# A windowed-attention and SwiGLU kernel on one core: loads reordered, later values cast by their DMA, attention steps on a fixed grid

## The chip, the cores and the metric

The kernel runs on one core of one Trainium2 chip. The metric is the device time of one execution in microseconds (us). Before the change three runs gave 435.56, 435.69 and 436.59 us; the median is 435.69 us.

## The reference

Eight batches of eight heads, 576 positions of 64 elements. Each query sees the keys within 32 positions, the eight positions in `global_idx` see all keys and are seen by all queries. The output rows of the attention go through a gated feed-forward block (FFN).

```python
scores = scale * np.matmul(q, k.transpose(0, 1, 3, 2))
mask = np.abs(pos[:, None] - pos[None, :]) <= 32
mask = mask | is_global[:, None] | is_global[None, :]
attn = softmax(np.where(mask, scores, -1e9))
x = np.matmul(attn, v).transpose(0, 2, 1, 3).reshape(4608, 512)
g = x @ w_gate
out = ((g / (1 + np.exp(-g))) * (x @ w_val)) @ w_out
```

## The kernel before

All matmuls are in bf16. The program writes its instructions in the order in which each engine executes them; each engine takes its own in that order, and a semaphore wait holds everything behind it on that engine.

**FFN.** The 4608 tokens are taken in nine chunks of 512. A chunk is 16 units: twelve `gate` units (four matmuls of 128x512 with `wg_sb` into `pg`, four with `wv_sb` into `pv`, a tanh on ScalarE, two products on VectorE) and four `outp` units (twelve matmuls with `wo_sb` into `po`, a scaling on ScalarE, a store). The operand is `xT`, which the attention fills.

**Attention.** A batch is a list of steps. `step_T` (batches 0 and 1 alone) transposes a pair of heads of the loaded `k_bf`, `q_bf` on TensorE into `kT`, `qT`. `step_GT`, `step_S2`, `step_SG`, `step_P2T`, `step_AV2` treat the global rows and columns: they need `kqm`, the gathered rows of the eight global positions. `step_S(u)` computes a band of scores, its exponential (ScalarE) and its product with the band mask (VectorE, `pt`). `step_AV(tp)` multiplies 128 rows of probabilities with the values (`va`, and `vb`, the values shifted by 64 rows, and `gvt` from `step_AV2`) and normalises on VectorE; `step_X(tp)` transposes the result into `xT`. `step_AV8` and `step_X8` do the last 64 rows.

**PSUM.** `psc` (tag "sc") and `pm` (tag "m") hold one pair of banks each, `pf` (tag "f") four single banks. `step_S`, `step_S2`, `step_SG` use `psc`; `step_AV` uses `pm`.

**Loads.** GpSimd issues the DMAs that cast from fp32 to bf16: `k_bf`, `q_bf`, the weights, and from batch 2 on `cast_qk`, which writes `kf`, `qf` to DRAM. It also issues the indirect gathers `kg`, `qg`, and `gather_mask` multiplies these into `kqm`. Each DMA of GpSimd waits for its eighth predecessor to land. The values come through SyncE as fp32 (`load_v` into `vst`) and GpSimd casts them (`cast_v`, line 108) into `va_bufs[b % 2]`. SyncE also issues `transpose_qk` (DMA transposes of `kf`, `qf` into `kT`, `qT`, lines 122 and 126), `load_vb` (lines 133, 134, a copy of `va` to `vb`) and the output stores (line 630).

**Order around the change.** The opening (lines 652 to 657) is batch 0 but for its last three steps. Then each chunk c takes the steps of batch c + 1, and `interleave` spreads them over the chunk by the units' estimated durations; `cast_qk`, `transpose_qk`, `load_v`, the gather and `cast_v` of later batches hang on units 1, 3, 5, 6 and 9 of each chunk.

Of the kernel before, what the change touches and what calls it, by code (L numbers as in the profile page):

```python
# [17 lines left out]
P = 128  # L18
# [8 lines left out]
def kernel(  # L27
# [63 lines left out]
    def v_block(u):  # L91
        return (WIN if u == 0 else 0), (P - WIN if u == 4 else P), P * u - WIN

    def load_v(b):
        vst = ldp.tile([P, 5, H, D], FP32, tag="vst", name="vst")
        vs = v[b].rearrange("h s d -> s h d")
        r = []
        for u in range(5):
            lo, hi, t0 = v_block(u)
            r.append(nc.sync.dma_start(out=vst[lo:hi, u], in_=vs[t0 + lo : t0 + hi]))  # L100
        return vst, r

    def cast_v(b, vst):
        va = va_bufs[b % 2]
        for u in range(5):
            lo, hi, _ = v_block(u)
            for a, z in ((lo, 64), (64, hi)) if u == 0 else ((lo, hi),):
                nc.gpsimd.tensor_copy(out=va[a:z, u, :, 0:D], in_=vst[a:z, u])  # L108

    flat = {}  # L110

    def cast_qk(b):
        for name, src in (("k", k), ("q", q)):
            t = dram.tile([S, H, D], BF16, name=f"{name}f{b}")
            nc.gpsimd.dma_start(out=t, in_=src[b].rearrange("h s d -> s h d"))
            flat[name, b] = t
# [116 lines left out]
    def gather_mask(kg, qg):  # L233
        kqm = gw.tile([P, 2, 2, D], BF16, tag="kqm", name="kqm")
        for a, src in ((0, kg), (1, qg)):
            nc.gpsimd.tensor_tensor(
                out=kqm[:, a], in0=bc(src, [[0, 2], [1, D]]),
                in1=bc(mka[:, a, :], [[1, 2], [0, D]]), op=ALU.mult,
            )
        return kqm  # L240

    vsts = [None] * B
    vsts[0], ins = load_v(0)
    for f in first:
        tc.add_manual_dep(
            ins[0].ins, f.ins.name,
# [10 lines left out]
    def load_wgv(i):  # L257
# [15 lines left out]
        out=band, in_=band, compare_op=ALU.is_ge, fill=0.0,  # L273
        base=2 * WIN, pattern=[[1, 64]], channel_multiplier=-1,
    )
    kqms[0] = gather_mask(*g0)
    cast_v(0, vsts[0])
    load_wgv(0)
    load_wgv(1)
    loaded[1] = new_qk()  # L280
    load_qk_part(1, loaded[1], 0)
    load_qk_part(1, loaded[1], 1)
    load_wgv(2)
    for i in range(4):
        nc.gpsimd.dma_start(
            out=wo_sb[:, 3 * i : 3 * i + 3, :],
            in_=moe_w_out[3 * P * i : 3 * P * (i + 1), :].rearrange("(fc p) m -> p fc m", p=P),
        )
    kqms[1] = gather_mask(*gather(1))


    mg = const.tile([P, S], BF16)
# [28 lines left out]
    def attention(b):  # L321
# [11 lines left out]
        def step_T(hp):  # L333
            if hp == 0:
                qTs[b] = bp.tile([P, HP, S], BF16, tag="qT", name="qT")
            if b > 0:
                pair = pm.tile([P, 2, 1024], BF16, tag="m", name="ps_t")
            for n, name in enumerate(("k", "q")):
                if b == 0:
                    ps = pf.tile([P, LJ, LP], BF16, tag="f", name="ps_t")  # L340
                else:
                    ps = pair[:, n, 0:S].rearrange("p (j i) -> p j i", j=LJ)
                src = ld[name]
                for j in range(LJ):
# [212 lines left out]
        def vb():  # L557
            st["vb"] = load_vb(b)

        L = lambda f, *a: (lambda: f(*a))  # L560
        if b == 0:
            return [
                L(step_T, 0), L(step_T, 1), tables, L(step_S, 0), L(step_T, 2), L(step_T, 3),
                L(step_GT), L(step_S2), L(step_SG), vb, L(step_P2T), L(step_S, 1),
                L(step_AV2), L(step_S, 2), L(step_AV, 0), L(step_S, 3), L(step_X, 0),
                L(step_AV, 1), L(step_X, 1), L(step_AV, 2), L(step_X, 2), L(step_AV, 3),
                L(step_X, 3),
            ], [[L(step_S, 4)], [L(step_AV8)], [L(step_X8)]]
        if b == 1:
            head = [  # L570
                [L(step_T, 0)], [L(step_T, 1)], [L(step_T, 2), vb], [L(step_T, 3)],
                [L(step_GT)],
            ]
        else:
            head = [[L(step_GT), vb]]
        return [], head + [
            [L(step_S2)],
            [L(step_SG)],
            [L(step_P2T), L(step_S, 0)],
# [58 lines left out]
    def interleave(units, steps):

        total = sum(d for d, _ in units)  # L640
        t = 0.0
        i = 0
        for d, f in units:
            f()
            t += d
            while i < len(steps) and (i + 0.5) * total <= t * len(steps):
                for g in steps[i]:
                    g()
                i += 1
        assert i == len(steps)  # L650

    head, rest = attention(0)
    for f in head:
        f()
    vsts[1], _ = load_v(1)
    cast_v(1, vsts[1])
    cast_qk(2)
    for c in range(NT // CH):
        steps = rest
        rest = []  # L660
        if c + 1 < B:
            steps += attention(c + 1)[1]
        units = ffn(CH * c, CH)

        def at(i, f, *a):
            d, g = units[i]
            units[i] = (d, lambda: (g(), f(*a)))

        if c + 2 < B:
            def raw(b):  # L670
                vsts[b], _ = load_v(b)

            def rows(b):
                kqms[b] = gather_mask(*gather(b))

            if c + 3 < B:
                at(1, cast_qk, c + 3)
            at(3, transpose_qk, c + 2)
            at(5, raw, c + 2)
            at(6, rows, c + 2)  # L680
            at(9, lambda b: cast_v(b, vsts[b]), c + 2)
        interleave(units, steps)


# [28 lines left out]
```

## Time and profile before

| | us |
|---|---|
| median of three runs | 435.69 |
| the profiled execution's own time | 433.27 |
| its span, first to last instruction | 431.6 |
| busy: TensorE, VectorE, ScalarE, GpSimd | 361.5, 238.9, 161.8, 96.3 |

A row of the profile names the source line, the engine (PE is TensorE, PEld its weight loads, DVE VectorE, ACT ScalarE, POOL GpSimd, SPq the queue of SyncE), the operation and the tiles as out<-in. The 40 digits of a slice line cover the span in equal parts of 10.8 us. PEclk is the granted TensorE clock: 1.00 is 2.4 GHz and 0.50 is 1.2 GHz. The difference between the own time and the span, 1.7 us, lies outside of the instructions.

### The profile page before, as it was taken

The page shows a single profiled execution, that of the slowest core. Times are in us where ns is not written, and L with a number is a line of the kernel's source. Part 1 is how long each engine was busy: PE and PEld are TensorE (multiplying, and loading weights), DVE is VectorE, ACT ScalarE, POOL GpSimd, SP SyncE. Part 2 cuts the span into 40 slices and gives each one's busy share as a digit, 9 for nine tenths or more (in the row PEclk, how much of TensorE's full clock was granted, in tenths as well). Part 3 has the DMA queues.
Part 4 walks back from the last instruction along what each step waited for, and adds up shares of the span by engine and source line. Part 5 has one row for each costly group of instructions (what it writes and reads, how often), then busy time and mean ns, then how long its engine had stood idle before and what let it go on. Part 6 is the DMA issues. An engine that isn't in the chain of part 4 may idle for free. (4 is left out here: it accounts for less than half of the span.)

```text
span 431.6 us, 7877 instructions
## 1 busy us (share of the span) xinstructions
PE 361.5 (84%) x3221; PEld 180.3 (42%) x3274; DVE 238.9 (55%) x467; ACT 161.8 (37%) x258; POOL 96.3 (22%) x122
## 2 busy tenths in 40 slices
PE   2668758028799989899899899898989998999996
PEld 2443323014344444454455444444444454444442
DVE  6554637004278538853884488358826862871760
ACT  3432424004354436333542355345435542322321
POOL 6642148127108200710270033003000000000000
PEclk9999979559999999999999999999999999999999
DMA  8999949998995939794989590168012001002002
GB/s 128 149 191 192 199 86 110 158 200 88 177 200 71 120 99 199 75 123 116 211 58 116 130 190 8 71 146 152 2 73 76 2 3 73 24 0 97 2 1 97
DMA packets 136147, 45.47 MB, mean 105 GB/s; under 512 B 122544, under 2 KB 130224, under 8 KB 136112
## 3 DMA queue, kind: packets, MB, share of 16 engines
q0 software_dynamic: 63968, 14.68, 36.3%
q1 hardware_dynamic: 72144, 30.29, 33.2%
q8 instruction: 25, 0.41, 0.4%
q14 instruction: 10, 0.08, 0.1%
HBM read 38.28 MB, written 16.52 MB: 127 GB/s over the span
## 5 line engine op out<-in xcount | busy, mean ns | idle before, releaser
L604 PE MATMUL pg<-xT,wg_sb 128*128 128x512 bf16 x402 | 109.9, 387 | 3.8 <-issue 2.2
L604 PE MATMUL pv<-xT,wv_sb 128*128 128x512 bf16 x425 | 111.8, 385 | 0.2
L610 ACT ACTIVATE th<-pg 128x512 bf16<-128x512 f32 x108 | 64.6, 598 | 115.2 <-PE pg L604 102.7
L612 DVE SCALAR_TENSOR_TENSOR gv<-th,pg 128x512 bf16<-128x512 bf16 x108 | 74.0, 685 | 56.0 <-ACT th L610 55.8
L623 PE MATMUL po<-wo_sb,h 128*128 128x512 bf16 x416 | 95.3, 379 | 2.2 <-issue 2.1
L616 DVE TENSOR_TENSOR h<-gv,pv 128x512 bf16<-128x512 bf16 x108 | 74.3, 688 | 11.8 <-PE pv L604 0.8
L604 PEld LDWEIGHTS <-wv_sb 128*128 128x128 bf16 x432 | 42.9, 99 | 52.8 <-issue 3.2
L623 PEld LDWEIGHTS <-h 128*128 128x128 bf16 x432 | 40.0, 98 | 45.6
L108 POOL CAST va<-vst 128x512 bf16<-128x512 f32 (+3 forms) x48 | 31.2, 659 | 122.2 <-DMA vst<-in_v_dram 88.9
L628 ACT ACTIVATE osb<-po 128x512 f32<-128x512 f32 x36 | 21.5, 597 | 91.4 <-PE po L623 71.9
L604 PEld LDWEIGHTS <-wg_sb 128*128 128x128 bf16 x432 | 37.3, 99 | 42.5 <-issue 7.0
L465 DVE TENSOR_TENSOR pt<-pe,band 128x1024 bf16<-128x1024 bf16 (+1 forms) x40 | 26.0, 651 | 35.3 <-ACT pe L460 35.2
L460 ACT ACTIVATE pe<-ps_s 128x1024 bf16<-128x1024 f32 (+1 forms) x40 | 37.8, 944 | 9.6 <-PE ps_s L452 9.6
L477 DVE TENSOR_REDUCE den<-ps_av 128x8 f32<-128x16 f32 (+1 forms) x40 | 6.8, 170 | 60.0 <-PE ps_av L504 37.8
L504 PE MATMUL ps_av<-vb,pt 128*64 128x66 bf16 x256 | 18.6, 202 | 19.9 <-DMA vb<-va 19.9
L504 PEld LDWEIGHTS <-pt 128*64 128x64 bf16 x512 | 18.6, 118 | 20.4 <-DMA vb<-va 18.9
L483 DVE TENSOR_TENSOR xa<-ps_av,den 128x512 bf16<-128x512 f32 (+1 forms) x40 | 25.5, 638 | 1.4
L541 ACT COPY xT<-ps_x 128x512 bf16<-128x512 bf16 x32 | 18.7, 583 | 18.5 <-PE ps_x L535 18.5
L495 PE MATMUL ps_av<-gvt,pg 128*64 128x264 bf16 x128 | 18.8, 305 | 7.6 <-DVE gvt L437 7.3
L535 PE MATMUL ps_x<-ident,xa 128*128 128x128 bf16 x128 | 13.4, 231 | 7.0 <-DVE xa L483 7.0
L504 PE MATMUL ps_av<-va,pt 128*64 128x66 bf16 x256 | 18.8, 202 | 0.0
L452 PE MATMUL ps_s<-qT,kT 64*128 64x64 bf16 x576 | 16.3, 197 | 1.8 <-DVE mg L311 1.0
(92 smaller groups left out, 224.0 us busy)
## 6 DMA issues: line engine op xcount, KB each, us to landing
out_dram<-osb SPq DMA_DIRECT2D x36, 256.0 KB, 2.0
vst<-in_v_dram SPq DMA_DIRECT2D x24, 256.0 KB, 6.3
vb<-va SPq DMA_DIRECT2D x16, 264.0 KB, 4.0
kf<-in_k_dram POOLq DMA_DIRECT2D x6, 576.0 KB, 8.3
qf<-in_q_dram POOLq DMA_DIRECT2D x6, 576.0 KB, 10.9
vst<-in_v_dram SPq DMA_DIRECT2D x16, 192.0 KB, 5.5
wg_sb<-in_moe_w_gate_dram POOLq DMA_DIRECT2D x3, 512.0 KB, 12.8
wv_sb<-in_moe_w_val_dram POOLq DMA_DIRECT2D x3, 512.0 KB, 15.4
```

The lines of the kernel that those rows point to most:

```text
L108: nc.gpsimd.tensor_copy(out=va[a:z, u, :, 0:D], in_=vst[a:z, u])
L460: nc.scalar.activation(out=pe, in_=ps[:, :, 0 : 64 * ns].rearrange("p r (s c) -> p r s c", c=64), func=AF.Exp, scale=SCALE,)
L465: nc.vector.tensor_tensor(out=pt.rearrange("p r s c -> p (r s) c"), in0=pe.rearrange("p r s c -> p (r s) c"), in1=bc(band, [[0, 2 * ns], [ ...
L483: nc.vector.tensor_tensor(out=xa.rearrange("p (g h) d -> p g h d", g=g), in0=bc(ps, pst + [[1, D]]), in1=bc(den, [[4, g], [1, 4], [0, D]]) ...
L495: nc.tensor.matmul(out=ps[64 * e : 64 * e + 64, hg], lhsT=st["pg"][:, P * tp + 64 * e : P * tp + 64 * e + 64], rhs=st["gv"].rearrange("p h ...
L504: nc.tensor.matmul(out=ps[64 * e : 64 * e + 64, hg, hl, :], lhsT=pt[:, hl % 2, 4 * (hl // 2) + 2 * (tp % 2) + e, :], rhs=(va if e == 0 els ...
L604: nc.tensor.matmul(out=ps[:, 0:n], lhsT=w[:, cc, P * fc : P * (fc + 1)], rhs=xT[:, cc, t0 : t0 + n], start=(cc == 0), stop=(cc == NCC - 1),)
L610: nc.scalar.activation(out=th[:, 0:n], in_=pg[:, 0:n], func=AF.Tanh, scale=0.5)
L612: nc.vector.scalar_tensor_tensor(out=gv[:, 0:n], in0=th[:, 0:n], scalar=1.0, in1=pg[:, 0:n], op0=ALU.add, op1=ALU.mult,)
L616: nc.vector.tensor_tensor(out=st["h"][:, fc, 0:n], in0=gv[:, 0:n], in1=pv[:, 0:n], op=ALU.mult)
L623: nc.tensor.matmul(out=po, lhsT=st["h"][:, fc, P * ts : P * (ts + 1)], rhs=wo_sb[:, fc, :], start=(fc == 0), stop=(fc == NFC - 1),)
L628: nc.scalar.mul(out=osb, in_=po, mul=0.5)
```

## The change

The values of batch 0 keep their way (`load_v0`, `cast_v0`), but the first gather mask and two weight loads stand between the casts. From batch 1 on `load_v` is five DMAs on GpSimd's queue that cast on the way into `va_bufs`; `vst` and the GpSimd casts are gone there. The gather of batch 1 is issued ahead of the second weight pair, `load_v(1)` behind the third, `cast_qk(2)` behind the output weights. `step_T` of batch 1 takes its PSUM pair from `psc` for three of four head pairs, and odd `step_AV` of batch 0 take theirs from `psc`. The opening runs all four `step_S` of batch 0 ahead of `step_GT`. `interleave` is replaced by a table `gaps`: gap n stands behind unit n of the whole program, and one step (a few pairs) goes into each; batch 1 fills gaps 0 to 15, batches 2 to 7 follow from gap 16 on at a pitch of 1.14 units.

```diff
+    def cast_v0(vst, us):
+        for u in us:
...
+    def load_v(b):
+        va = va_bufs[b % 2]
+        vs = v[b].rearrange("h s d -> s h d")
+        for u in range(5):
+            lo, hi, t0 = v_block(u)
+            nc.gpsimd.dma_start(out=va[lo:hi, u, :, 0:D], in_=vs[t0 + lo : t0 + hi])
...
+    cast_v0(vst0, range(0, 3))
     kqms[0] = gather_mask(*g0)
-    cast_v(0, vsts[0])
+    cast_v0(vst0, range(3, 4))
     load_wgv(0)
+    cast_v0(vst0, range(4, 5))
+    g1 = gather(1)
     load_wgv(1)
     loaded[1] = new_qk()
     load_qk_part(1, loaded[1], 0)
     load_qk_part(1, loaded[1], 1)
+    kqms[1] = gather_mask(*g1)
     load_wgv(2)
+    load_v(1)
...
-    kqms[1] = gather_mask(*gather(1))
+    cast_qk(2)
...
-                pair = pm.tile([P, 2, 1024], BF16, tag="m", name="ps_t")
+                pool, tag = (pm, "m") if hp == 3 else (psc, "sc")
+                pair = pool.tile([P, 2, 1024], BF16, tag=tag, name="ps_t")
...
-            full = pm.tile([P, 2, 512], FP32, tag="m", name="ps_av")
+            pool, tag = (psc, "sc") if b == 0 and tp % 2 else (pm, "m")
+            full = pool.tile([P, 2, 512], FP32, tag=tag, name="ps_av")
...
+        def later():
+
+            if b + 2 < B:
+                transpose_qk(b + 2)
+                kqms[b + 2] = gather_mask(*gather(b + 2))
+            if b + 3 < B:
+                cast_qk(b + 3)
+
+        def later_v():
+            if b + 2 < B:
+                load_v(b + 2)
...
+                L(step_T, 0), L(step_T, 1), tables, L(step_S, 0), L(step_S, 2),
+                L(step_T, 2), L(step_T, 3), L(step_S, 1), L(step_S, 3),
+                L(step_GT), L(step_S2), L(step_SG), vb, L(step_P2T), L(step_AV2),
+                L(step_AV, 0), L(step_AV, 1), L(step_X, 0), L(step_AV, 2), L(step_X, 1),
+                L(step_AV, 3), L(step_X, 2), L(step_X, 3),
+            ], [L(step_S, 4)], [L(step_AV8), later_v], [L(step_X8)]
...
-            [L(step_X, 2), L(step_S, 4)],
+            [L(step_X, 2), L(step_S, 4), later],
...
-            [L(step_AV8)],
+            [L(step_AV8), later_v],
...
+    for i, g in enumerate([s4, av8, x8, []]):
+        gaps[i] = g + tops[i]
+    for i, g in enumerate(core[:12]):
+        gaps[4 + i] = g
+    gaps[8].append(lambda: transpose_qk(2))
+    gaps[9].append(lambda: kqms.__setitem__(2, gather_mask(*gather(2))))
+    gaps[10].append(lambda: cast_qk(3))
...
+    for i, g in enumerate(order):
+        gaps[16 + int(i * 1.14)] = g
...
+        for f in ffn(c * CH, CH):
+            f[1]()
+            for g in gaps.get(n, []):
+                g()
+            n += 1
```

Three places of the order. First SyncE's queue from the values of batch 0 to the first stores, before the change (the number behind kf, qf is the batch; va0 and vb_391 belong to batch 0, va1 and vb_833 to batch 1):

```order
L133 DMA vb_391<-va0_95 64x2112
L134 DMA vb_391<-va0_95 64x2112
L100 DMA vst_619<-in_v_dram 96x8x64
L100 DMA vst_619<-in_v_dram 128x8x64 x3
L100 DMA vst_619<-in_v_dram 96x8x64
L122 DMA_TRANSPOSE kT0_97<-kf2_631 128x4x576
L126 DMA_TRANSPOSE qT_762<-qf2_633 128x4x576
L133 DMA vb_833<-va1_96 64x2112
L134 DMA vb_833<-va1_96 64x2112
```

and now, where the last va0 and vb_1417 belong to batch 2:

```order
L140 DMA vb_463<-va0_95 64x2112
L139 DMA vb_841<-va1_96 64x2112
L140 DMA vb_841<-va1_96 64x2112
L128 DMA_TRANSPOSE kT0_97<-kf2_218 128x4x576
L132 DMA_TRANSPOSE qT_1048<-qf2_220 128x4x576
L652 DMA out_0_dram<-osb_1199 128x512
L652 DMA out_0_dram<-osb_1241 128x512
L128 DMA_TRANSPOSE kT1_98<-kf3_1140 128x4x576
L132 DMA_TRANSPOSE qT_1264<-qf3_1142 128x4x576
L652 DMA out_0_dram<-osb_1290 128x512
L652 DMA out_0_dram<-osb_1332 128x512
L139 DMA vb_1417<-va0_95 64x2112
```

The shifted values of batch 1 moved ahead of the transposes of batch 2; those of batch 2 stand behind the transposes of batch 3.

Second, GpSimd from the third weight pair (`wg_sb`, `wv_sb`) to the casts for batch 2 (`kf`), before:

```order
L259 DMA wg_sb<-in_moe_w_gate_dram 128x4x512
L259 DMA wv_sb<-in_moe_w_val_dram 128x4x512
L285 DMA wo_sb<-in_moe_w_out_dram 128x3x512 x4
L226 DMA kg<-in_k_dram,gofs 128x64
L226 DMA qg<-in_q_dram,gofs 128x64
L236 TENSOR_TENSOR kqm<-kg,mka 128x128
L236 TENSOR_TENSOR kqm<-qg,mka 128x128
L108 CAST va_96<-vst 32x8x64
L108 CAST va_96<-vst 64x8x64
L108 CAST va_96<-vst 128x8x64 x3
L108 CAST va_96<-vst 96x8x64
L115 DMA kf_631<-in_k_dram 4608x1x64
```

and now (the gather of batch 1 has been issued ahead of the second weight pair):

```order
L242 TENSOR_TENSOR kqm<-kg,mka 128x128
L242 TENSOR_TENSOR kqm<-qg,mka 128x128
L264 DMA wg_sb<-in_moe_w_gate_dram 128x4x512
L264 DMA wv_sb<-in_moe_w_val_dram 128x4x512
L114 DMA va_96<-in_v_dram 96x8x64
L114 DMA va_96<-in_v_dram 128x8x64 x3
L114 DMA va_96<-in_v_dram 96x8x64
L295 DMA wo_sb<-in_moe_w_out_dram 128x3x512 x4
L121 DMA kf_218<-in_k_dram 4608x1x64
```

The mask of batch 1 moved from behind the output weights to ahead of the third weight pair, and six casts became five DMAs.

Third, ScalarE in the opening (kT copies belong to `step_T`, pe to `step_S`, p2e, pge, p2t to the global steps, xT to `step_X`), before:

```order
L296 ACTIVATE iq<-iq,ngcol 128x640
L460 ACTIVATE pe<-ps_s 128x1024
L352 COPY kT_97<-ps_t 128x576 x2
L402 ACTIVATE p2e<-ps_s_365 128x640
L384 ACTIVATE pge<-ps_sg 128x576
L416 COPY p2t<-ps_p2t 128x640
L460 ACTIVATE pe<-ps_s 128x1024 x3
L541 COPY xT<-ps_x 128x4x128 x4
```

and now:

```order
L306 ACTIVATE iq<-iq,ngcol 128x640
L471 ACTIVATE pe<-ps_s 128x1024 x2
L363 COPY kT_97<-ps_t 128x576 x2
L471 ACTIVATE pe<-ps_s 128x1024 x2
L413 ACTIVATE p2e<-ps_s_437 128x640
L395 ACTIVATE pge<-ps_sg 128x576
L427 COPY p2t<-ps_p2t 128x640
L553 COPY xT<-ps_x 128x4x128 x4
```

Three exponentials moved ahead of the global steps.

## Rows read from the trace of the kernel before

**Rows 1.** The page: its head, and the granted clock in 40 slices.

```profile
span 431.6 us, 7877 instructions
...
PEclk9999979559999999999999999999999999999999
```

**Rows 2.** Waits of TensorE, 0 to 117 us: who <- for whom: us in total, times, longest.

```profile
PE ps_av L504 <- DMA vb<-va: 19.9, 1, 19.9
PE ps_x L535 <- DVE xa L483: 7.0, 6, 1.3
...
PE ps_g L366 <- POOL kqm L236: 3.6, 1, 3.6
```

**Rows 3.** Timeline of SyncE's queue around 80 us: start, duration, instruction.

```profile
72.57 5.76 SPq L122 DMA_TRANSPOSE kT<-kf  x1
78.44 6.44 SPq L126 DMA_TRANSPOSE qT<-qf  x1
84.98 0.54 SPq L133 DMA_DIRECT2D vb<-va  x1
```

**Rows 4.** Timeline of GpSimd around 60 us; in brackets the idle time before and its end.

```profile
59.77 0.39 POOL L236 TENSOR_TENSOR kqm<-kg,mka 128x128 bf16<-128x128 f32 x1 [13.50 <-DMA kg<-in_k_dram,gofs]
...
60.59 3.85 POOL L108 CAST va<-vst 32x512 bf16<-32x512 f32 x6
64.39 2.28 POOL L115 DMA_DIRECT2D kf<-in_k_dram  x1
```

**Rows 5.** Timeline of TensorE in the opening.

```profile
14.74 0.46 PE L366 MATMUL ps_g<-ident,kqm 128*128 128x128 bf16 x2
...
22.50 0.43 PE L495 MATMUL ps_av<-gvt,pg 128*64 128x264 bf16 x2 [1.04 <-DVE gvt L437]
...
33.51 0.61 PE L535 MATMUL ps_x<-ident,xa 128*128 128x128 bf16 x4 [1.27 <-DVE xa L483]
```

**Rows 6.** Timeline of ScalarE in the opening: the first exponential.

```profile
12.78 1.02 ACT L460 ACTIVATE pe<-ps_s 128x1024 bf16<-128x1024 f32 x1 [2.92 <-PE ps_s L452]
```

**Rows 7.** Timeline of TensorE in chunks 0 and 1.

```profile
34.78 0.59 PE L604 MATMUL pg<-xT,wg_sb 128*128 128x512 bf16 x1 [0.67 <-ACT xT L541]
...
55.61 1.03 PE L604 MATMUL pv<-xT,wv_sb 128*128 128x512 bf16 x4
...
116.97 0.81 PE L604 MATMUL pg<-xT,wg_sb 128*128 128x512 bf16 x3
...
132.51 0.30 PE L495 MATMUL ps_av<-gvt,pg 128*64 128x264 bf16 x2 [0.86 <-DVE gvt L437]
```

**Rows 8.** The chain that ended last: chunk 7 begins, one pv group, chunk 8 begins.

```profile
365.34 0.86 PE pg L604 x4
366.20 0.86 PE pv L604 x4
...
396.42 0.86 PE pg L604 x4
```

**Rows 9.** Waits of TensorE, 117 to 366 us (chunks 1 to 6).

```profile
PE ps_av L495 <- DVE gvt L437: 5.6, 6, 1.2
PE ps_av L516 <- ACT xT L541: 5.6, 6, 0.9
```

**Rows 10.** One line's durations (ns min/median/max): line 437 to 30 us, then lines 437 and 465, 117 to 366 us.

```profile
L437 DVE TENSOR_TENSOR gvt<-lo,gvt x1: 195/195/195, 22.3 to 22.3; 128x8 bf16<-128x8 f32 x1
...
L437 DVE TENSOR_TENSOR gvt<-lo,gvt x6: 195/462/466, 132.0 to 339.3; 128x8 bf16<-128x8 f32 x6
...
L465 DVE TENSOR_TENSOR pt<-pe,band x30: 424/692/1062, 128.6 to 356.1; 128x1024 bf16<-128x1024 bf16 x24, 128x512 bf16<-128x512 bf16 x6
```

**Rows 11.** DMA traffic: all, 19 to 53 us; GB/s in 40 slices, 137.5 to 147.6 and 127.2 to 134.5 us.

```profile
DMA packets 10152, 6.62 MB, mean 195 GB/s; under 512 B 4894, under 2 KB 10021, under 8 KB 10149
...
GB/s 0 0 2 41 65 96 84 137 154 153 158 152 157 159 157 160 157 160 157 153 155 155 160 157 160 156 160 156 160 156 160 157 161 156 257 124 66 8 0 0
...
GB/s 209 230 220 265 271 252 324 223 223 230 222 217 218 66 15 10 15 15 36 104 180 192 252 285 251 154 97 146 180 243 237 126 84 17 15 15 10 0 0 0
```

More of the change, by code (lines that the diff above doesn't have):

```diff
@@ L92, in v_block, with load_v0 @@
         return (WIN if u == 0 else 0), (P - WIN if u == 4 else P), P * u - WIN
-    def load_v(b):
+    def load_v0():
         vst = ldp.tile([P, 5, H, D], FP32, tag="vst", name="vst")
-        vs = v[b].rearrange("h s d -> s h d")
+        vs = v[0].rearrange("h s d -> s h d")
         r = []
@@ L101, in load_v @@
         return vst, r
-    def cast_v(b, vst):
-        va = va_bufs[b % 2]
-        for u in range(5):
+    def cast_v0(vst, us):
+        for u in us:
             lo, hi, _ = v_block(u)
             for a, z in ((lo, 64), (64, hi)) if u == 0 else ((lo, hi),):
-                nc.gpsimd.tensor_copy(out=va[a:z, u, :, 0:D], in_=vst[a:z, u])
+                nc.gpsimd.tensor_copy(out=va_bufs[0][a:z, u, :, 0:D], in_=vst[a:z, u])
+    def load_v(b):
[4 more added lines that the diff above has]
+            nc.gpsimd.dma_start(out=va[lo:hi, u, :, 0:D], in_=vs[t0 + lo : t0 + hi])
     flat = {}
@@ L240, in gather_mask @@
         return kqm
-    vsts = [None] * B
-    vsts[0], ins = load_v(0)
+    vst0, ins = load_v0()
     for f in first:
@@ L562, in attention @@
             return [
[L563 to L576, printed above, removed]
+                L(step_T, 0), L(step_T, 1), tables, L(step_S, 0), L(step_S, 2),
[4 more added lines that the diff above has]
+            ], [L(step_S, 4)], [L(step_AV8), later_v], [L(step_X8)]
+        core = [
             [L(step_S2)],
@@ L585, in attention @@
             [L(step_AV, 2)],
-            [L(step_X, 2), L(step_S, 4)],
+            [L(step_X, 2), L(step_S, 4), later],
             [L(step_AV, 3)],
             [L(step_X, 3)],
-            [L(step_AV8)],
+            [L(step_AV8), later_v],
             [L(step_X8)],
         ]
+        if b == 1:
+            return [
+                [L(step_GT)], [L(step_T, 0)], [L(step_T, 1)], [L(step_T, 2), L(step_T, 3), vb],
+            ], core
+        return [[L(step_GT), vb]] + core
     def ffn(t0, n):
@@ L635, in ffn @@
         ]
[L638 to L652, printed above, removed]
+    head, s4, av8, x8 = attention(0)
     for f in head:
         f()
-    vsts[1], _ = load_v(1)
-    cast_v(1, vsts[1])
-    cast_qk(2)
-    for c in range(NT // CH):
[L659 to L682, printed above, removed]
+    tops, core = attention(1)
+    gaps = {}
+    for i, g in enumerate([s4, av8, x8, []]):
[5 more added lines that the diff above has]
+    gaps[10].append(lambda: cast_qk(3))
+    due = {1: 16}
+    order = core[12:]
+    for b in range(2, B):
+        steps = attention(b)
+        due[b] = len(order) + 2 * ((512 - 64 * b + P - 1) // P) + 4
+        order += steps
+    for i, g in enumerate(order):
+        gaps[16 + int(i * 1.14)] = g
+    for b in range(2, B):
+        assert 16 + int(due[b] * 1.14) < 16 * b, (b, due[b])
+    n = 0
+    for c in range(NT // CH):
+        for f in ffn(c * CH, CH):
[3 more added lines that the diff above has]
+            n += 1
+    assert max(gaps) < n
 _INS = ['q', 'k', 'v', 'global_idx', 'moe_w_gate', 'moe_w_val', 'moe_w_out']
```

## The prediction

> **What bounds the kernel now.** I read the head of the page and its clock line first [rows 1], then TensorE's waits in two stretches [rows 2, 9], then the timelines of the queues behind the longest wait [rows 3, 4], and last the chain that ended last [rows 8]. The chain shows that TensorE is the bound where nothing disturbs it: chunk 7, without attention, runs from 365.34 to 396.42, so 31.1 us, and a gate unit takes 0.86 + 0.86 = 1.73 us. Four outp units are what is left of 31.1 after twelve gates, 10.3 us. Nine chunks are 280 us of the span; the rest is opening, attention and waits.
>
> The waits lie mostly ahead of 117 us. TensorE waits 19.9 us for `vb`, 7.0 us in six pieces for `xa` and 3.6 us for `kqm` [rows 2]. The clock line falls to half in the slices around 80 and 90 us [rows 1], so what follows the long stall also starts at 1.2 GHz. SyncE shows why `vb` is late: it stands behind the two transposes of batch 2, which start at 72.57 and 78.44, and is issued at 84.98 [rows 3]. They had waited for `kf`, which GpSimd issued at 64.39 only because its gather landed at 59.77 and its casts stood ahead [rows 4]. So an order of queues costs the time, not the amount of work.
>
> **The opening, 0 to the first gate at 34.78.** S(2) now follows S(0) at once, but both need the one `psc` pair, so S(2) waits for the exponential of S(0), 1.02 us from 12.78 [rows 6], and so do S(1) and S(3) later. Two score steps of 0.6 us and two such waits ahead of `step_GT` give it a start near 20.0 instead of 14.74 [rows 5]; its copy on VectorE then queues behind the product of S(3), near 21.8, so `step_S2` starts near 22.1, some 6.0 us later than now. The way from there to the first AV loses the two score steps that stood in it, -0.8. From the first AV at 22.50 to the end of the last X at 34.1 it takes 11.6 us now, with four waits for `xa` of up to 1.27 [rows 5]. With two pairs the normalisation of one AV lies beside the next AV: four AVs of 0.85 (slow clock), four X of 0.55, and one wait at the end make 6.7, so -4.9. Net +0.3. I bound it by -3.5 (the exponentials hide wholly behind the transposes) and +2 (one more wait per score step). The mask of batch 0 stands behind three casts now; `step_GT` comes 5 us later too, which hides it; without that cover it would cost about 1 us.
>
> **Chunk 0, 34.78 to 116.97, 82.2 us** [rows 7]. From 34.78 to 56.6 (the gate at 55.61 with its 1.03) run seven units, the tail of batch 0 and all of `step_T` of batch 1, 21.9 us; I keep that. To it come five gates (8.65), four outp (10.3), and the attention of batch 1. A later batch costs (365.34 - 116.97) / 6 - 31.1 = 10.3 us, of which 11.2 / 6 = 1.9 are the waits of [rows 9]; 8.4 remain, plus 0.9 for `gvt` and about 0.7 where the last X now stands right ahead of the first gate of chunk 1 (the 0.67 at 34.78 is the same wait). Sum 51.0, if every load is in time: a gain of 31.2. The waits say the same: 19.9 + 3.6 + some 3.5 of `xa` inside the chunk leave 4 us for the half clock.
>
> Are they in time? The queue moved 195 GB/s of landed bytes from 19 to 53 us [rows 11]. The first weight DMA starts some 1.5 us earlier than now, near 17.5. Behind it stand six weight DMAs of 512 KB, `vb` of batch 0 (528 KB), keys and queries of batch 1 (1152 KB) and the values as bf16 (576 KB): 5.4 MB, 28 us, so `va` near 49 and `vb` near 53. It is needed after unit 8, near 62. The mask of batch 1 is done near 30, needed at 37; the keys near 40, needed from 41 for the first half (which lands near 37); the third weight pair near 46, needed at 60; the output weights (1.6 MB more) near 57, needed at 71. All have 4 us or more. The GpSimd casts that go (3.85 us of issue, [rows 4]) were off the path; the five DMAs in their place are too.
>
> **Chunks 1 to 6.** AV8 waits 5.6 us in six times for the copy of X3, because both stand in one gap now [rows 9]. On the new grid each step has a gap of its own, and a unit of at least 1.73 us covers 0.93: -5.6. AV(0) waits 5.6 us for `gvt`. From 16 + int(1.14 i), one unit stands between AV2 and AV(0) for batches 2, 4, 5 (a gate), 6 and 7 (an outp, longer and without VectorE work), two for batch 3; so three waits of 0.93 go. The other three shrink. In the steady chunks the last operation of `gvt` takes 462 ns in the median, 195 ns in the opening, and the slowest `pt` ahead of it 1062 instead of 692 [rows 10]; both fall on the GpSimd casts of values, which the change removes. That is 0.27 + 0.37 = 0.64 for each: -1.9. Together -4.7. The Trainium skill names a reason (GPSIMD Engine Reference, Specifications): GpSimd shares its SBUF interfaces with VectorE, in contention with instructions that have two SBUF inputs. These two have, and the trace agrees; by the page the wait stays short only while GpSimd computes nothing.
>
> **What is late next.** `vb` of batch 2 now stands behind the transposes of batch 3 and two stores. The casts of keys and queries move 160 GB/s [rows 11], 3.7 us for 576 KB. `kf`, `qf` of batch 2 follow the output weights, to 64.5; the values of batch 2, the gather and two transposes share the engines until about 76; the mask, in order on GpSimd, lets the casts for batch 3 go near 76.5. A cast lands 8.2 us after its issue (64.39 to 72.57, [rows 3, 4]); so 84 and 88, then the transposes until 92 to 95 (5.8 to 6.4 us of issue when crowded, [rows 3]), `vb` issued near 93 to 97, landed 97 to 103. AV(0) of batch 2 comes 132.51 - 116.97 = 15.5 us into chunk 1 now [rows 7], about 17.8 with one more gate and two steps of batch 1 ahead, so near 103. I take 1 us, with bounds 0 and 7 (5 us of stall and the half clock behind it). From batch 3 on casts run a batch ahead, and these waits have over 10 us to spare.
>
> Cost nothing: the new PSUM pair of `step_T` (its wait is inside one pair), the stores (three buffers of `osb`), the tail.
>
> **Sum** against the profiled execution's 433.27: +0.3 - 31.2 - 5.6 - 4.7 + 1 = -40.2, so 393.1. That execution was 2.4 us under the median of the three runs, 435.69; on that scale 395.5.
>
> **The rivals.**
> 1. `vb` of batch 2 is late. For it: three queues have to meet inside 5 us of slack. Deciding point: it lands after 103. Six us more than forecast, 401 to 403. The Trainium skill has a rule that makes it likelier (DMA: Bandwidth & Descriptors, Specifications): pieces under 512 B miss line rate, through a read-modify-write. The values now go in pieces of 128 B, before 256. The rows: fp32 values moved near 225 GB/s, so 5.2 us for a batch, casts of the same pieces 160 GB/s, so 3.7 [rows 11]; against the rule's direction the halved bytes win. Were the cast values to cost twice, two batches would shift `vb` by 7 us: 403.
> 2. The steady gain does not come: waits for `gvt` and `xT` give way to others at the same places. Then 10.3 us stay: 406. Against it: their cause is adjacency, which is gone.
> 3. The opening really gains: 391 to 392.
> 4. The change does not do what it says: `va` of batch 1, last in the one casting queue, still lands after 62. At 66 it costs 4 us and the half clock, 401. Against it: 28 us of bytes at a rate that held for 34 us.
> 5. Slower than before: values, keys, queries and gathers of each batch in one queue, behind a mask that waits on GpSimd, so that each AV(0) waits for `vb`. It decides from 40.2 / 6 = 6.7 us per batch, 436 and up. Against it: a batch moves 3 x 3.7 = 11 us of casts in an interval of about 40.
>
> **How the numbers follow.** Forecast 0.60, rival 1 0.19, rival 2 0.10, rival 3 0.06, rival 4 0.04, rival 5 0.01. The range: below, 395.5 - 3.8 (opening) - 1 (`vb`) - 0.9 (rest of the `gvt` waits) - about 1 = 389; above, rivals 1 and 4 and most of rival 2, 406. A measurement here can tell 0.3%, about 1.3 us, from no change. Only rival 5 is not faster: 0.98 faster, 0.01 same, 0.01 slower.
>
> **What would show it.** TensorE's waits to 86 us should hold no `vb` and no `kqm` wait over 1 us; the first gate stands near 35, chunk 1 begins near 86 and the clock line stays at 9 from there. AV8 no longer waits for `xT`; `gvt` totals about 1 us; `pt` and `gvt` show no long versions. If the starts of chunks 1 to 7 stand some 39 us apart (14 of 15 steps in each), the grid works. I am wrong if a DMA wait of some us stands ahead of AV(0) of batch 1 or 2, or if the first gate lies off 35 by more than 3.

## The result and the profile after

Four runs of the changed kernel took 392.73 to 393.64 us, median 392.96; four of the kernel before 435.56 to 436.59, median 435.63. The ratio is 0.902, with an interval of 0.900 to 0.904: faster by 42.7 us. The profiled execution took 393.64 us, 39.6 less than the profiled one before.

| stretch, us, profiled executions | before | after | difference |
|---|---|---|---|
| to the first gate | 34.78 | 35.12 | +0.3 |
| chunk 0 | 82.19 | 49.65 | -32.5 |
| start of chunk 1 to the end of the span | 314.6 | 307.1 | -7.5 |

The head of the page after the change and its clock line, against [rows 1]:

```profile
span 391.9 us, 7880 instructions
...
PEclk9998999999999999999999999999999999999999
```

The two slices at 5 are gone. Chunk 0 shows what they and the waits were worth, in windows of the kernel before and of the changed one (stretch, length, then busy us of PE, PEld, DVE, ACT and POOL, granted clock, DMA share, GB/s):

```profile
34.78:116.97 82.19, 49.46 (x476) 23.80 (x484) 30.74 (x58) 21.58 (x35) 31.50 (x33) 0.83 1.30 147
```

```profile
35.12:84.77 49.65, 44.99 (x471) 21.91 (x471) 29.14 (x55) 21.34 (x34) 24.26 (x23) 0.97 1.67 177
```

TensorE's idle time in the chunk falls from 32.7 to 4.7 us, and for almost the same matmuls it is busy 4.5 us less, at a clock of 0.97 instead of 0.83. (Before, rows of some matmuls are missing, 476 for 484 weight loads; 1.2 us of the idle time are their gaps.) TensorE's waits to 86 us, against [rows 2], and from 86 us to the end, against [rows 9]:

```profile
PE ps_s L463 <- ACT pe L471: 2.2, 2, 1.1
...
PE pg L626 <- ACT xT L553: 1.7, 2, 1.0
...
PE ps_x L547 <- DVE xa L494: 1.5, 4, 0.6
```

```profile
PE ps_av L507 <- DVE gvt L448: 1.7, 3, 0.7
PE ps_av L516 <- DMA vb<-va: 0.8, 1, 0.8
PE ps_x L547 <- DVE xa L494: 0.4, 2, 0.2
```

The 19.9 us for `vb` and the 3.6 for `kqm` are gone, `xa` has fallen from 7.0 to 1.5, AV8's wait for `xT` from 5.6 to nothing, `gvt` from 5.6 in six to 1.7 in three. New are 2.2 us in the opening, where the score steps share one PSUM pair and wait for the exponentials, 1.0 us for `xT` at the start of chunk 1 (the other 0.7 stands at the first gate, as before), and 0.8 us for `vb` of batch 2.

The timeline of TensorE in the opening, in chunk 0 and at the starts of chunks 1, 3, 4 and 5, against [rows 5, 7]:

```profile
20.14 0.40 PE L377 MATMUL ps_g<-ident,kqm 128*128 128x128 bf16 x2
...
27.73 0.43 PE L507 MATMUL ps_av<-gvt,pg 128*64 128x264 bf16 x2 [1.11 <-DVE gvt L448]
...
35.12 1.86 PE L626 MATMUL pg<-xT,wg_sb 128*128 128x512 bf16 x4 [0.68 <-ACT xT L553]
...
62.81 0.30 PE L507 MATMUL ps_av<-gvt,pg 128*64 128x264 bf16 x2 [0.60 <-DVE gvt L448]
...
84.77 1.02 PE L626 MATMUL pg<-xT,wg_sb 128*128 128x512 bf16 x4 [0.99 <-ACT xT L553]
86.59 0.30 PE L528 MATMUL ps_av<-gvt,pg 128*64 128x264 bf16 x2
...
165.62 1.04 PE L626 MATMUL pg<-xT,wg_sb 128*128 128x512 bf16 x4
...
204.90 1.04 PE L626 MATMUL pg<-xT,wg_sb 128*128 128x512 bf16 x4
...
244.39 1.04 PE L626 MATMUL pg<-xT,wg_sb 128*128 128x512 bf16 x4
```

Chunk 3 (from 165.62) takes 39.3 us and chunk 4 (from 204.90) 39.5. The row at 86.59 is AV8 of batch 1, which stood ahead of chunk 1 before; it and X8 take 0.36 and 0.12 us. SyncE's queue, against [rows 3]; `vb` of batch 1 is the first pair, of batch 2 the last:

```profile
49.44 0.46 SPq L139 DMA_DIRECT2D vb<-va  x1
49.99 0.55 SPq L140 DMA_DIRECT2D vb<-va  x1
63.28 5.91 SPq L128 DMA_TRANSPOSE kT<-kf  x1
69.31 6.34 SPq L132 DMA_TRANSPOSE qT<-qf  x1
...
85.16 3.93 SPq L128 DMA_TRANSPOSE kT<-kf  x1
89.19 3.21 SPq L132 DMA_TRANSPOSE qT<-qf  x1
92.49 1.01 SPq L652 DMA_DIRECT2D out_dram<-osb  x2
93.66 0.47 SPq L139 DMA_DIRECT2D vb<-va  x1
94.22 1.09 SPq L140 DMA_DIRECT2D vb<-va  x1
```

`vb` of batch 1 is issued 13 us ahead of its use (AV(0), 62.81 above). Before, it was issued at 84.98 [rows 3], 11 us behind the start of AV(0), and then had to land:

```profile
73.70 0.30 PE L495 MATMUL ps_av<-gvt,pg 128*64 128x264 bf16 x2 [0.60 <-DVE gvt L437]
...
93.98 0.21 PE L504 MATMUL ps_av<-vb,pt 128*64 128x66 bf16 x1 [19.95 <-DMA vb<-va]
```

That of batch 2 is tight. A piece of the chain that ended last, and the row of TensorE that it releases:

```profile
94.22 9.53 DMA vb<-va
```

```profile
103.80 0.22 PE L516 MATMUL ps_av<-vb,pt 128*64 128x66 bf16 x1 [0.79 <-DMA vb<-va]
```

Last, two lines of VectorE in the later chunks (ns min/median/max), against [rows 10]:

```profile
L448 DVE TENSOR_TENSOR gvt<-lo,gvt x6: 195/196/197, 102.4 to 314.5; 128x8 bf16<-128x8 f32 x6
...
L476 DVE TENSOR_TENSOR pt<-pe,band x30: 425/691/746, 99.0 to 332.0; 128x1024 bf16<-128x1024 bf16 x24, 128x512 bf16<-128x512 bf16 x6
```

The long versions (462 and 1062 ns) are gone.

### The profile page after: what moved, and what is told of

It is laid out like the page before. It is cut to its first block, busy times and chain, and to the rows that moved or that the text cites. A ratio compares the mean times of both kernels' runs of the same rounds, so it can differ in the third digit from the quotient of the medians.

```text
span 391.9 us, 7880 instructions
## 1 busy us (share of the span) xinstructions
PE 361.7 (92%) x3274; PEld 176.7 (45%) x3274; DVE 236.9 (60%) x467; ACT 163.1 (42%) x258; POOL 99.2 (25%) x115
## 4 chain that ended last, share of the span: by engine, by line
PE 80%; DVE 8%; ACT 5%; DMA 2%; POOL 2%; issue 2%; SPq 0%; DVEq 0%; ACTq 0%; POOLq 0%
PE po L645 25%; PE pg L626 22%; PE pv L626 20%; PE ps_s L463 3%; ACT pe L471 3%; PE ps_av L507 3%; DMA vb<-va 2%; PE ps_x L547 2%; PE ps_av L516 2%; DVE pt L476 2%; DVE h L638 1%; DVE gv L634 1%; DVE xa L494 1%; DVE gvt L440 1%; PE ps_s L406 1%
## 5 line engine op out<-in xcount | busy, mean ns | idle before, releaser
L626 PE MATMUL pg<-xT,wg_sb 128*128 128x512 bf16 x432 | 112.3, 383 | 1.7 <-ACT xT L553 1.7
L645 PE MATMUL po<-wo_sb,h 128*128 128x512 bf16 x432 | 98.4, 380 | 0.0
L114 POOL DMA_DIRECT2D va<-in_v_dram x35 | 32.8, 1202 | 102.6 <-PE ps_av L516 79.7
L507 PE MATMUL ps_av<-gvt,pg 128*64 128x264 bf16 x128 | 18.5, 299 | 3.4 <-DVE gvt L448 3.4
L463 PEld LDWEIGHTS <-kT 64*128 64x128 bf16 x576 | 11.5, 98 | 11.8 <-issue 8.7
```

The lines of the kernel that those rows point to most:

```text
L114: nc.gpsimd.dma_start(out=va[lo:hi, u, :, 0:D], in_=vs[t0 + lo : t0 + hi])
L463: nc.tensor.matmul(out=ps[:, par, 64 * slot : 64 * slot + 64], lhsT=kT[r : r + 64, hp, 64 * t : 64 * t + P], rhs=qTs[b][r : r + 64, hp, 64 ...
L507: nc.tensor.matmul(out=ps[64 * e : 64 * e + 64, hg], lhsT=st["pg"][:, P * tp + 64 * e : P * tp + 64 * e + 64], rhs=st["gv"].rearrange("p h ...
L626: nc.tensor.matmul(out=ps[:, 0:n], lhsT=w[:, cc, P * fc : P * (fc + 1)], rhs=xT[:, cc, t0 : t0 + n], start=(cc == 0), stop=(cc == NCC - 1),)
L645: nc.tensor.matmul(out=po, lhsT=st["h"][:, fc, P * ts : P * (ts + 1)], rhs=wo_sb[:, fc, :], start=(fc == 0), stop=(fc == NFC - 1),)
```

## The experiments

Each was run beside the kernel before on one chip; ratios are to that kernel. The chips are three, and the kernel before took 435.56, 438.67 and 433.88 us on them in the median (experiments 1 to 3 and the first run of 4; 5; the rest), so differences of some us between groups are not read without a run from the same chip. Three take one idea alone into the kernel before, the others change the kernel after. The whole output is computed in all of them.

**1. The order of SyncE's queue alone, in the kernel before.** The transposes and the value load of chunk 0 are moved behind the shifted values of batch 1.

```diff
-            at(3, transpose_qk, c + 2)
-            at(5, raw, c + 2)
+            at(3 if c else 9, transpose_qk, c + 2)
+            at(5 if c else 9, raw, c + 2)
```

> The kernel before, with one thing of the change: in chunk 0 the transposes of batch 2 and the load of the values of batch 2 are issued behind the shifted values of batch 1 on SyncE's queue. Every load, cast and step is otherwise as before. My theory (the order of SyncE's queue made the 19.9 us wait): the casts of batch 1 end near 64.4 us, vb is issued at once and lands near 69, ahead of its use at 73.7; the wait of 19.9 us goes with about 1.5 us of half clock: 414 us (412 to 417). Rival (the loads themselves are late, the opening has too many bytes in flight): vb still lands 10 us or more after 74, and the time stays above 425 us. Either way the 3.6 us for kqm stay.

Measured: 417.06 us against 435.56, ratio 0.958 (0.954 to 0.961), so -18.5. The wait for `vb` is gone. Its waits of TensorE from 34 to 102 us, the rows around the second of them, and the tile `osb` (who waited for its DMAs):

```profile
PE ps_g L366 <- POOL kqm L236: 3.3, 1, 3.3
PE ps_g L366 <- ACT xT L552: 3.0, 1, 3.0
```

```profile
100.69 0.27 PE L366 MATMUL ps_g<-ident,kqm 128*128 128x128 bf16 x2 [2.95 <-ACT xT L552]
...
101.91 1.91 PE L604 MATMUL pv<-xT,wv_sb 128*128 128x512 bf16 x4
```

```profile
L630 SPq DMA_DIRECT2D out_dram<-osb x4: 332/386/715, 95.7 to 100.4; - x4
...
  ACT osb L628: 7.3, 1
```

What stands late next is the output: the stores of chunk 0 are now behind the transposes and the value load, ScalarE waits 7.3 us for an `osb` buffer, its copy to `xT` waits behind that, and TensorE loses 3.0 us and then runs slower (granted clock 0.61 from 100.70 to 104.00). By the starts of the chunks in the two traces, chunk 0 takes 21.2 us less and chunk 1 takes 4.7 more. So one move on one queue is worth less than half of the change, and less than the 21.6 us that I expected, because the same queue then holds something else.

**2. The casts of values moved away from the attention's VectorE work, in the kernel before.** Their loads move too, behind the first store of the chunk.

```diff
-            at(5, raw, c + 2)
+            at(12, raw, c + 2)
-            at(9, lambda b: cast_v(b, vsts[b]), c + 2)
+            at(13, lambda b: cast_v(b, vsts[b]), c + 2)
```

> The kernel before, with the fp32 values of a later batch loaded behind the first store of its chunk instead of behind the transposes, so that the GpSimd casts fall beside the outp units and not beside AV2. Theory (casts and VectorE compete): the last operation of gvt falls from 462 to about 196 ns in the median, the longest pt of the steady chunks from 1062 to under 800 ns, the waits of AV(0) for gvt from 5.6 to about 2.4 us in chunks 1 to 6 (0.64 us in five of six): 432.4 us (431.5 to 434). Rival (the wait is one of place in VectorE's queue alone): gvt waits stay over 5 us and the time stays at 435.6 plus or minus 1.

Measured: 432.22 against 435.56, ratio 0.995 (0.991 to 0.998), -3.3. Waits of TensorE from 117 us on, and the two lines of VectorE:

```profile
PE ps_av L516 <- ACT xT L541: 5.6, 6, 0.9
PE ps_av L495 <- DVE gvt L437: 3.6, 6, 0.6
```

```profile
L437 DVE TENSOR_TENSOR gvt<-lo,gvt x6: 196/196/197, 132.1 to 337.8; 128x8 bf16<-128x8 f32 x6
...
L465 DVE TENSOR_TENSOR pt<-pe,band x30: 425/692/694, 128.7 to 354.7; 128x1024 bf16<-128x1024 bf16 x24, 128x512 bf16<-128x512 bf16 x6
```

With the order of the steps unchanged and only the loads and casts elsewhere, the last `gvt` operation falls from 462 to 196 ns, the slowest `pt` from 1062 to 694, and the waits for `gvt` from 5.6 to 3.6: 2.0 us, 0.33 each where I had worked out 0.64 from the two lines. The 1062 was the wrong figure to add to each wait: of the six `pt` just ahead of a `gvt` it is this one alone, the others take 0.68 to 0.69 us.

```profile
171.99 1.06 DVE L465 TENSOR_TENSOR pt<-pe,band 128x1024 bf16<-128x1024 bf16 x1
```

In the two traces chunks 1 to 6 together are 1.4 us shorter; what makes up the rest of the 3.3 between the medians is not shown. That casts beside them slow these two operations is shown; through what, is not. The Trainium skill names a contention of GpSimd with VectorE instructions that have two SBUF inputs (GPSIMD Engine Reference, Specifications). Both operations have two, and the trace agrees with it.

**3. The grid alone, in the kernel before.** In chunks 1 to 6 one list entry goes behind each unit, in place of `interleave`.

```diff
-        interleave(units, steps)
+        if c == 0:
+            interleave(units, steps)
+        else:
+            for i, (_, f) in enumerate(units):
+                f()
+                for g in steps[i] if i < len(steps) else []:
+                    g()
```

> The kernel before, with the attention steps of chunks 1 to 6 on a fixed grid, one list entry behind each unit, and nothing else changed (chunk 0 as before, casts where they were). Theory (adjacency makes the wait of AV8 for the copy of X3): that wait, 5.6 us in six times, is gone, the waits for gvt stay near 5.6: 430 us (429 to 431.5). Rival (the steady gain does not come, the waits move to other places): the waits of TensorE in chunks 1 to 6 keep their sum of 11 us, 435 to 436 us.

Measured: 431.93 against 435.56, ratio 0.992 (0.989 to 0.995), -3.6. Its waits of TensorE from 118 us on:

```profile
PE ps_av L495 <- DVE gvt L437: 4.5, 6, 1.1
PE ps_x L535 <- DVE xa L483: 2.2, 12, 0.3
```

AV8's 5.6 us for `xT` are gone, so adjacency was their cause. But 2.2 us for `xa` came in their place, at one entry per unit with an X one unit behind its AV. (The view also holds 0.9 us for X8 of batch 1, at 118.51; that wait stands at 116.63 in the kernel before and is not new.) By the waits that makes -5.6 - 1.1 (`gvt`) + 2.2 = -4.5. In the two traces chunks 1 to 6 together are 3.0 us shorter, so 1.5 of it went elsewhere, which I have not traced.

**4. The values as fp32 through SyncE again, in the kernel after.** The load of batch b+2 stands behind AV8 of batch b, its GpSimd cast behind `step_S2` of batch b+1 (`load_v` and `cast_v` as before the change; those of batches 1 and 2 stand earlier). `cast_qk(2)` moves too, behind the opening and the casts of batch 1.

```diff
-            nc.gpsimd.dma_start(out=va[lo:hi, u, :, 0:D], in_=vs[t0 + lo : t0 + hi])
+            nc.sync.dma_start(out=vsts[b][lo:hi, u], in_=vs[t0 + lo : t0 + hi])
```

> The changed kernel, with the values of batches 1 to 7 loaded as fp32 by SyncE and cast on GpSimd again, in an order that keeps vb of batch 1 ahead of the transposes. Theory (the casting queue brings little by itself beyond the contention): vb of batch 1 is still in time, gvt's last operation is back near 460 ns where casts fall beside it, the waits for gvt grow by 0.64 us in three to five batches: 395.5 us (394 to 398). Rival 1 (the casting queue was what brought the values in time): a wait of several us for va or vb of batch 1 or 2, over 400 us. Rival 2 (it brings nothing): 393 plus or minus 0.7.

Measured: 412.77 against 435.56, ratio 0.947 (0.943 to 0.950): 17 us more than expected. The first wait of TensorE from 95 us on, and SyncE's queue:

```profile
PE ps_av L522 <- DMA vb<-va: 14.9, 1, 14.9
```

```profile
99.05 11.91 SPq L114 DMA_DIRECT2D vst<-in_v_dram  x5
111.00 1.83 SPq L147 DMA_DIRECT2D vb<-va  x1
```

My placement did that: the load of batch 3's values stood ahead of batch 2's `vb`, the fault of experiment 1 once more. So the run says nothing of the price of casts, and I ran it again with the later loads (now of batch b+1) and casts moved behind:

```diff
-            [L(step_S2)],
+            [L(step_S2), later_v],
-            [L(step_X, 0), L(step_S, 2)],
+            [L(step_X, 0), L(step_S, 2), later_cast],
```

> The changed kernel with the values of batches 1 to 7 loaded as fp32 by SyncE and cast on GpSimd, as in the earlier run of this kind, but with each later load issued behind vb of the batch before, so that no load of values stands ahead of a vb on SyncE's queue. Theory (that run lost its 19 us to this place alone; the casting queue itself is worth little): the wait of 14.9 us is gone, about 1.5 us of wait for vb of batch 1 stays, 396 us (394.5 to 398). Rival 1 (fp32 values through SyncE are late wherever they stand): over 400 us with a DMA wait of several us. Rival 2 (no cost at all): 393.3 or less.

Measured: 399.76 (396.70 to 400.68) against 433.88, ratio 0.922 (0.920 to 0.923). The profiled execution, the fastest, took 396.70; in it the wait for `vb` of batch 2 is 2.2 us, not 0.8, and the last `gvt` operation takes 195 to 198 ns. So this way of bringing the values costs 3 us to 7 us against the kernel after; I had expected about 3. The longer wait comes by GpSimd's queue: the casts for batch 2 are issued there at 57.00 instead of 48.90, behind the casts of values, those for batch 3 at 80.00 instead of 76.28, and so the transposes, with `vb` behind them, start 3.4 us later than in the kernel after (85.16 there):

```profile
88.60 4.03 SPq L136 DMA_TRANSPOSE kT<-kf  x1
```

What costs the other executions up to 4 us more I can't say, as none of them was profiled; their mean granted clock is 0.987 to 0.996, against 1.000 in the one above.

**5. The opening.** The kernel after, and three openings, on one chip. A gate is that of one profiled execution, and for one program it moves by about 1 us (35.12 above, 36.00 here), so the medians decide. First the kernel itself again:

> The changed kernel once more, as the measure for the runs beside it on the same chip: 393.0 plus or minus 0.7, first gate near 35.1 us, vb of batch 2 landing near 103.7 us and keeping TensorE waiting about 0.8 us.

Measured: 393.60 (392.22 to 393.71); its first gate stands at 36.00. Then it with the order and casts of the opening before, and one pair for AV:

```diff
-                L(step_T, 0), L(step_T, 1), tables, L(step_S, 0), L(step_S, 2),
-                L(step_T, 2), L(step_T, 3), L(step_S, 1), L(step_S, 3),
-                L(step_GT), L(step_S2), L(step_SG), vb, L(step_P2T), L(step_AV2),
...
+                L(step_T, 0), L(step_T, 1), tables, L(step_S, 0), L(step_T, 2), L(step_T, 3),
+                L(step_GT), L(step_S2), L(step_SG), vb, L(step_P2T), L(step_S, 1),
+                L(step_AV2), L(step_S, 2), L(step_AV, 0), L(step_S, 3), L(step_X, 0),
...
```

> The changed kernel with the opening of the kernel before: its step order, one PSUM pair for all AV steps, and casts and mask of batch 0 in the old order. Theory (the new opening nets nothing: what the two pairs give back, the four score steps ahead of the global steps take): first gate at 34.8 us instead of 35.1, and the time the same as the changed kernel within 0.7 us, 393. Rival (the new opening is a real part of the gain): first gate at 38 us or later and 396 or more.

Measured: 394.65 (394.09 to 396.16), first gate 36.55, in an execution whose queries of batch 0 came 0.6 us later than in the one above. Then only the second pair taken away:

```diff
-            pool, tag = (psc, "sc") if b == 0 and tp % 2 else (pm, "m")
+            pool, tag = pm, "m"
```

> The changed kernel with one PSUM pair for the AV steps of batch 0, the step order of its opening kept. Theory (the second pair alone is worth 4.9 us of opening, and 0.8 us come back since the wait for vb of batch 2 is set by the queues and not by TensorE): first gate near 40 us, waits of X for xa near 1.27 in four, no wait for vb of batch 2: 397 us (396 to 398). Rival (the second pair is worth nothing): 393.

Measured: 396.65 (396.40 to 397.33), first gate 38.82. Last, the order before with the second pair, AV(2) right behind AV(1):

```diff
+                L(step_AV2), L(step_S, 2), L(step_AV, 0), L(step_S, 3), L(step_X, 0),
+                L(step_AV, 1), L(step_AV, 2), L(step_X, 1), L(step_AV, 3), L(step_X, 2),
```

> The changed kernel with an opening that should be shorter: the step order of the kernel before, but AV(2) of batch 0 takes the psc pair and stands right behind AV(1), so that the last three X steps wait less. Theory: first gate near 31.5 us, 3.5 us earlier; but the time hardly moves, 392 to 393, because vb of batch 2 still lands near 103 to 104 us behind two transposes and two stores on SyncE's queue, and the wait for it grows from 0.8 to about 4 us. Rival (what bounds the opening bounds the whole): 389.5 us, the wait for vb stays under 1.5 us.

Measured: 392.00 (391.40 to 392.30), first gate at 33.44:

```profile
33.44 1.87 PE L624 MATMUL pg<-xT,wg_sb 128*128 128x512 bf16 x4 [0.67 <-ACT xT L551]
```

So in the changed order the second pair gives 3.05 us, and without it the 0.8 us for `vb` of batch 2 are gone as well, so the pair itself is worth about 3.9 by estimate. The opening as a whole nets 1.05: the order of the steps takes the rest back, with the score steps ahead of `step_GT` (20.30 in the repeat, 15.70 in the order before). The order of the casts changed with it, but no wait of TensorE in the opening names them. The pair with the order before nets 2.65. I had expected the gate at 31.5 and a wait of 4 us for `vb` of batch 2 to give that back. Both were off: the gate came 1.9 later, and `vb` kept TensorE waiting for 1.0, so the 392.0, though as forecast, came about otherwise.

**6. What is late next.** In the kernel after, the transposes of batch 3 go behind `vb` of batch 2.

```diff
-                transpose_qk(b + 2)
+                if b > 1:
+                    transpose_qk(b + 2)
...
+        if b == 2:
+            return [[L(step_GT), vb, L(transpose_qk, 3)]] + core
```

> The changed kernel with vb of batch 2 issued ahead of the transposes of batch 3 on SyncE's queue, and nothing else. Theory (the one DMA wait left is a matter of that order): the wait of 0.8 us for vb goes, the transposes of batch 3 have 40 us to spare, 392.4 us (391.8 to 393.2), 0.8 under the changed kernel. Rival (the engines are simply full there, whatever stands first): vb lands at the same 103 us, no gain.

Measured: 393.22 (391.56 to 394.12). The second copy of `vb` of batch 2 is issued at 84.78 instead of 94.22, and nothing waits for it:

```profile
84.78 0.55 SPq L140 DMA_DIRECT2D vb<-va  x1
```

In the traces chunk 1 takes 40.3 us instead of 41.4 (41.3 in the repeat); in the medians 0.8 us can't be told from no change. With the mixed opening of experiment 5 as well:

> The changed kernel with both: the step order of the old opening with AV(2) of batch 0 in the psc pair, and vb of batch 2 ahead of the transposes of batch 3. Theory (the gain of the opening was partly taken by the wait for vb): no wait for vb, first gate near 33.4 us, 390.9 us (390 to 391.8), under both kernels. Rival (the two do not add): 392 or more.

Measured: 389.82 (389.04 to 391.15) against 433.88, ratio 0.899 (0.897 to 0.901): all its runs are under the fastest of the kernel after (392.22, on another chip) and under the fastest of the run above, beside which it ran (391.56). Its first gate, and all its waits from 86 us on that name a releaser:

```profile
31.93 0.59 PE L627 MATMUL pg<-xT,wg_sb 128*128 128x512 bf16 x1 [0.67 <-ACT xT L551]
```

```profile
PE ps_av L505 <- DVE gvt L446: 1.7, 3, 0.6
PE ps_x L545 <- DVE xa L492: 0.4, 2, 0.2
```

No wait for a load is left in the steady part. This version is faster than the kernel before by 44 us, and by 3.4 than the run above, which differs from the kernel after by the place of `vb` alone. The same opening had its gate at 33.44 in experiment 5, so some 1.5 us of that difference vary between executions.

**7. The pitch.** The kernel after with one step behind every unit.

```diff
-        gaps[16 + int(i * 1.14)] = g
+        gaps[16 + int(i * 1.0)] = g
```

> The changed kernel with a pitch of 1.0 instead of 1.14 units, so that the attention of batches 2 to 7 is done half a chunk earlier and AV2 and AV(0) are always one gate apart. Theory (the pitch matters only through the waits for gvt): six waits of 0.6 us instead of three, 1.9 us more, 395 us (394 to 396), and no wait for xT at AV8. Rival 1 (pace does nothing): 393.0 to 393.7. Rival 2 (denser steps overload VectorE or ScalarE, so that PSUM comes free late): over 397.

Measured: 398.18 (396.27 to 398.55), ratio 0.916 (0.914 to 0.918): 5 us over the kernel after (and over the 393.22 of experiment 6 on the same chip), 3 more than I expected. Waits of TensorE from 86 us on:

```profile
PE ps_av L507 <- DVE gvt L448: 3.9, 6, 0.8
...
PE ps_x L547 <- DVE xa L494: 1.8, 11, 0.2
```

`gvt` is waited for in every batch again (+2.2) and X waits for its `xa` in eleven places (+1.4); `vb` is waited for 0.3 us less. That is 3.3 us of the 4.5 between the profiled executions; the rest I have not traced.

## Why the prediction was right

The time lies 2.5 us under the 395.5 forecast and inside the range. The sum itself was closer: 393.1 for the profiled execution, 393.64 measured. That it is so close is in part luck, since chunk 0 came out 0.9 us better and the later chunks 1.3 worse. The step that failed is the last, to the scale of the median: I added 2.4 us because the profiled execution before lay so far under its median, and the one after lies 0.7 above its own. Runs of the kernel before went from 433.6 to 440.3 us over the three chips, those of the kernel after only from 392.2 to 393.7 in two groups, so the step carried a scatter of the kernel before over to the one after.

- **Opening, +0.3:** the first gate at 35.12, forecast 35.1; `step_GT` 20.14 (20.0), first AV 27.73 (27.7). Put back into the kernel after, the opening before costs 1.05 in the median, so the change there is a small gain and not +0.3; both are inside the bounds. The stretch from the first AV to the end of the last X, 27.73 to 34.45, is the 6.7 us of my sum. But experiment 5 shows that of the 4.9 saved there about 3.9 are the pair's; the rest comes with the new order, in which S(3) no longer stands in that stretch.
- **Chunk 0, -31.2:** -32.5, of which AV8 and X8 of batch 1 are moved, not saved. So -32.1, 0.9 better. The 4 us that were left for the half clock are there: busy time fell by 4.5, of which 0.5 moved (by 1.2 more, if the gaps of the missing rows are counted as busy). Idle time fell by 28.0, of which the waits for `vb`, `kqm` and `xa` are 19.9, 3.6 and 3.2. Experiment 1 shows that moving `vb` alone gives 18.5 of the whole, net of the 4.7 that it loses in chunk 1. The rest of chunk 0 (the early mask, the pair for `step_T`, the stores) I did not run part by part.
- **AV8 behind X3, -5.6:** exact, and experiment 3 shows the cause.
- **`gvt`, -4.7:** measured -3.9. Both parts are there, but the second was mis-sized: 0.64 us a wait from two lines of VectorE, 0.33 in experiment 2, because the 0.37 for the slowest `pt` belongs to one batch of six. Three waits of 0.6 stay instead of three of 0.3, which is the 0.8 us missing.
- **`vb` of batch 2, +1:** issued 93.66, forecast 93 to 97; landed 103.75, forecast 97 to 103; needed 102.7; 0.8 us of wait. From issue to landing it took 9.5 us (the second copy), where I had 4 to 6. So it landed just behind the late end, and the stall stayed small because the issue came at the early end and the use at the time forecast.
- **Not in my sum:** 0.4 us for `xa` in the later chunks. With the 0.48 us that moved in, the later part gained 8.0 us like for like, where I had 9.3.

Of the rivals, 1 was close: `vb` did land after its deciding point of 103, but for 0.8 us, not 6; experiment 4 shows the same wait at 14.9. The values of batch 1 had landed by 49.99, when their second copy to `vb` goes out, near the 49 forecast. That 49 was partly luck: 17.5 + 28 is 45.5, and no row gives the other 3.5; the first weight DMA was issued at 18.41, and with part of the output weights 5.91 MB had landed by 49.5, at 190 GB/s. From 44.3 to 48.2 us 3961 of 4087 packets are under 512 B, and the slices of that stretch stand at some 155 GB/s, beside a mean of 199 from 40 to 44.3. So the 0.59 MB of the values took some 3.8 us by estimate, near the 3.7 of the prediction and not twice that. The Trainium skill's rule that pieces under 512 B miss line rate (DMA: Bandwidth & Descriptors, Specifications) agrees with the lower rate. Rival 2, that waits give way to others, came true in part for the grid alone in the kernel before (2.2 of 5.6 us) and for pitch 1.0, so the 1.14 is a part of the gain. Rival 3 is what the mixed opening does (392.0); this change gains only 1.05 there. Rival 4 fell with 13 us to spare, and rival 5 because no `vb` is waited for from batch 3 on.

The three parts tried in the kernel before give 18.5, 3.3 and 3.6 us, 25.4 of 42.7. The other 17 are not settled part by part; experiment 1 shows one way they hang together, since a load moved ahead put stores behind others until the rest of the queue was in order too.

## What to carry to other kernels

Read a long DMA wait on the queue that issued it: what stands ahead there, and what that waited for. When you reorder such a queue, name the next thing behind the moved ones (stores and their buffers included), for it took back 4.7 us here, and a load put ahead of a needed copy cost 14.9 in a careless variant. And judge a second buffer and a new order of steps apart: here the one paid for the other.

## What the runs showed of the hardware

- The clock in the opening differed between executions of the same program. Windows of the changed kernel around its first gate, in the execution above (us, PE busy, PEld, DVE, ACT, POOL, PEclk, DMA share, GB/s):

```profile
31.60:35.00 3.40, 1.86 (x38) 1.29 (x34) 2.04 (x6) 1.70 (x3) 1.14 (x3) 1.00 1.26 199
35.00:38.60 3.60, 3.48 (x8) 0.99 (x8) 0.69 (x1) 0.66 (x2) 2.53 (x3) 0.53 1.31 202
```

  TensorE had been granted 2.4 GHz while it was busy for 1.86 of 3.40 us, and ran the first unit near 1.2 GHz (0.53). In the repeat of experiment 5 the clock was 1.00 in the 4.4 us ahead of the gate, with 3.00 busy, and the first four matmuls took 1.02 instead of 1.86 us. So the gate stood 0.9 us later there, and yet chunk 1 began at 84.04, not at 84.77.
- The granted clock of the rows does not show every slow stretch. In the old and in the mixed opening of experiment 5 the first four matmuls took 1.87 us, as at 0.53 above, while the rows give 1.00 for 36.50 to 40.00 and 33.40 to 36.80. The duration of a group of known shape is the surer sign.
- In experiment 1 the clock fell after TensorE had been idle for 2.95 us: it was 0.61 from 100.70 to 104.00, and a pv group took 1.91 us instead of 1.03.
